# Score and value steps of a batch gathered into fewer visits, in banks borrowed from other stages

## The chip, the cores and the metric

One NeuronCore of a Trainium2 chip runs the whole kernel in one launch. The metric is the device time of that launch in microseconds; the median of several runs counts. The engines are named as in the profile: PE (TensorE) for matrix products and transposes, PEld for its weight loads, DVE (VectorE), ACT (ScalarE), POOL (GpSimd), and SP, whose queue issues most transfers.

## The reference

Two layers follow each other. The first is attention in a sliding window of 64 positions, causal, for 8 batches, 8 heads, 576 positions and a head size of 64. The second normalises the joined heads (512 wide), multiplies by two weight matrices with a relu between them, and adds its input.

```python
scores = scale * np.matmul(q, k.transpose(0, 1, 3, 2))
mask = (rel >= 0) & (rel < window)              # rel = query position - key position
attn = softmax(np.where(mask, scores, -1e9))
x = np.matmul(attn, v)                          # joined over heads: 8 x 576 x 512
xn = (x - mu) / np.sqrt(var + 1e-06) * g_ln
out = x + np.maximum(xn @ w_ch1, 0.0) @ w_ch2   # 512 -> 2048 -> 512
```

## The kernel before, in words

**Groups and stages.** The first 512 positions of each batch form a group of their own (groups 0 to 7); the last 64 positions of all eight batches, the tails, form group 8. For a group the second layer (the MLP) runs on TensorE in units: in groups 2 to 7 there are 16 units of the first layer (`l1`, L401: four matmuls of 128x512, then a relu on ScalarE, L405) and 14 half-products of the second layer (`stage`, L478: eight matmuls of 128x256 each). The second layer is computed with seven products instead of eight, in the order 1, 2, 6, 5, 7, 4, 3, two halves each. Product n's sums of the hidden values are made by VectorE (`s_sums`, L452), and what the products leave in three PSUM banks A, B and C is added by VectorE to the residual rows (`post`, L485). Bank A takes product 1, is added out, then takes product 6, is added out, then 7. Bank C lies in the transposing bank t1.

**The next batch's attention.** While the MLP of group g runs, the attention of batch g + 1 is computed in four blocks of 128 positions. For a block j there is a score step (`s_mm`): 16 matmuls (L286) on half of the rows of the array, into two PSUM banks, two exponentials on ScalarE (L294) and one multiplication by the mask on VectorE (`s_mask`, L301). Then a value step (`b_step`): 16 matmuls with 64 columns (L321) into a two-bank tile `xps`, and on VectorE a reciprocal (L324), a product (L327) and two statistics instructions (L329, L332). Then `z_step`: four GpSimd instructions (L351 to L354) that make the normalised rows z. Then `zt_step`: a transposing DMA on SP's queue (L362) or, for block 3 of batches 3 and 5, four transposes on TensorE (L366) and a copy on ScalarE. The tails have the same steps; in groups 3 and 5 one block of tails is handled, in group 7 two.

**Casts and transposes for the batch after that.** GpSimd casts the next but one batch's q and k to 16 bits (`cast_qk`, L128): in slot 11 two q casts and one k cast, in slot 16 the last k cast. The k casts are transposed on TensorE (`t_main`, L229, eight transposes each, through the banks t0 and t1, copied out by ScalarE at L215); the q casts are transposed by DMAs on SP's queue (L223). Then follow the casts of v (L147) and two DMAs issued by GpSimd that make a shifted copy of it.

**What sets the order.** The order is written out by hand. Each unit has a slot: after unit i has been issued, the calls registered for slot i are issued, in the order of registration. Every engine runs its own instructions in this order. The call `at(i, f, ...)` registers f in slot i. In groups 2 to 6 a batch's steps stand so (before):

- slot 27 of the group before: score step 0; slot 28: its mask
- slots 2, 7, 12: value step, rows and z of block 0, 1, 2, with score step 1, 2, 3 behind it; slots 3, 8, 13: masks
- slot 17: value step 3, its rows and z
- slots 1 and 5 in groups 3 and 5: score and value step of the tails
- slots 17 and 21 (18 and 22 in group 2): `t_main` for the two k casts
- slots 8 to 11 four `s_sums`, slots 13 to 15 six more, slots 19 and 21 one each

The PSUM has eight banks: two for scores (`sc`), two for the value step (`xps`), t0 and t1 for transposes, and two (`mm`) for the MLP, in which banks A and B lie as well.

Of the kernel before, what the change touches and what calls it, by code (L numbers as in the profile page):

```python
# [10 lines left out]
FP32 = mybir.dt.float32  # L11
# [4 lines left out]
ALU = mybir.AluOpType  # L16
# [4 lines left out]
def kernel(  # L21
# [10 lines left out]
    nc = tc.nc  # L32
    B, H, S, D = q.shape
# [3 lines left out]
    NGRP = B + 1  # L37
    NKC = DM // 128
    NHC = HID // 128
    NHP = H // 2  # L40
# [39 lines left out]
    tail32, tail16, tailT, vT = {}, {}, {}, {}  # L80
# [157 lines left out]
    def t_tail(i, x):  # L238
# [18 lines left out]
                    nc.tensor.transpose(out=tp[:, r, hp, :], in_=src[:, r, 2 * hp:2 * hp + 2, :], identity=ident16)  # L257
        evac(0, tailT[i][x], tp)

    def s_mm(g, j, pe_mask=False):  # L260
        sc = [ps_s.tile([128, NHP, 2, 64], FP32, tag="sc", name=f"sc_{g}_{j}_{par}") for par in range(2)]
        pt = p_pt.tile([128, 2, NHP, 2, 64], FP16, tag="pt", name=f"pt_{g}_{j}")
        pts[(g, j)] = pt
        if pe_mask:
            m = mbias[:, :]
            mb = bass.AP(tensor=m.tensor, offset=m.offset, ap=[m.ap[0], [0, NHP * 2], m.ap[1]])
            for par in range(2):
                nc.tensor.matmul(
                    out=sc[par][:, :].rearrange("p h w i -> p (h w) i"), lhsT=ident16, rhs=mb,
                    start=True, stop=False, skip_group_check=True,  # L270
                )
        for hp in range(NHP):
            for iw in range(2):
                for par in range(2):
                    rows = slice(64 * par, 64 * par + 64)
                    if g == NGRP - 1:
                        lhsT = tailT[j][1][rows, iw, hp, :]
                        rhs = tailT[j][0][rows, hp, 64 * iw:64 * iw + 64]
                    else:
                        w = 2 * j + iw  # L280
                        lhsT = qkT[g][1][rows, hp, 64 * w:64 * w + 128]
                        rhs = qkT[g][0][rows, hp, 64 * w:64 * w + 64]
                        if g >= XQ:
                            qb = flat(g)[rows, SM * hp + 16 * w:SM * hp + 16 * w + 16]
                            rhs = bass.AP(tensor=qb.tensor, offset=qb.offset, ap=[qb.ap[0], [128, 4], [1, 16]])
                    nc.tensor.matmul(out=sc[par][:, hp, iw, :], lhsT=lhsT, rhs=rhs,  # L286
                                     start=not pe_mask, stop=True, skip_group_check=pe_mask)

        for par in range(2):
            o, i = pt[:, par], sc[par][:, :]  # L290
            if XQ <= g < NGRP - 1:
                o = o.rearrange("p h w (r j) -> p (h w) r j", j=4)
                i = i.rearrange("p h w (j r) -> p (h w) r j", j=4)
            nc.scalar.activation(out=o, in_=i, func=AF.Exp, bias=0.0, scale=scale)  # L294
# [6 lines left out]
        nc.vector.tensor_tensor(out=ptv, in0=ptv, in1=mb, op=ALU.mult)  # L301

    def b_step(g, kb):
        kblk = f"{g}_{kb}"
        sfx, nb = ("r", 2) if g == NGRP - 1 else ("", None)
        if kb % 2 == 0:
            if (g, kb // 2) not in x_norm:
                for h in ((1, 0) if g // 2 == 2 else (0, 1)):
                    x_norm[(g, h)] = p_xn.tile([128, 2, DM], FP32, tag="xn" + sfx, name=f"xn_{g}_{h}", bufs=nb)
        xv = x_norm[(g, kb // 2)][:, kb % 2, :]  # L310
        xn = xv.rearrange("p (h d) -> p h d", h=H)
        xps = ps_x.tile([128, H, 128], FP32, tag="xps", name=f"xps_{kblk}")
        pt = pts.pop((g, kb))
        for h in range(H):
            par, hp = h % 2, h // 2
            for r in range(2):
                if sfx:
                    rhs = vT[kb][:, r, h, :]
                else:
                    rhs = (vA if r else vB)[g][:, kb, h, :]  # L320
                nc.tensor.matmul(out=xps[64 * r:64 * r + 64, h, :D + 1], lhsT=pt[:, par, hp, r, :], rhs=rhs,  # L321
                                 start=True, stop=True)
        rcp = p_blk.tile([128, H], FP32, tag="rcp", name=f"rcp_{kblk}")
        nc.vector.reciprocal(out=rcp, in_=xps[:, :, D])  # L324
        rcp_b = bass.AP(tensor=rcp.tensor, offset=rcp[:, :].offset,
                        ap=[rcp[:, :].ap[0], rcp[:, :].ap[1], [0, D]])
        nc.vector.tensor_tensor(out=xn, in0=xps[:, :, 0:D], in1=rcp_b, op=ALU.mult)  # L327
        stats = p_blk.tile([128, nc.vector.BN_STATS_DIM], FP32, tag="stats", name=f"stats_{kblk}")
        nc.vector.bn_stats(out=stats, in_=xv)  # L329
        if g not in mvg:  # L330
            mvg[g] = p_grp.tile([128, 4, 2], FP32, tag="mvg" + sfx, name=f"mvg_{g}", bufs=1 if sfx else 2)
        nc.vector.bn_aggr(out=mvg[g][:, kb, :], in_=stats)  # L332
        if g < 2 and (g, kb) != (0, 2):
            z_step(g, kb)
# [506 lines left out]
    for g in range(NGRP):  # L841
# [7 lines left out]
        def at(i, f, *a):  # L849
            slots[min(i, len(slots) - 1)].append((f, a))  # L850

        b = g + 1
        if g == 0:
            at(0, b_step, 0, 3)
# [28 lines left out]
        if g == 1:  # L883
            at(0, cast_qk, 2, 0)
            at(0, cast_qk, 2, 1)
            at(1, b_step, 1, 3)
            at(2, zt_step, 1, 2)
            at(13, newton, 1, 0, 4)
            at(5, zt_step, 1, 3)
            at(4, alloc_v, 2)  # L890
            at(4, alloc_qkT, 2)
            at(4, alloc_vB, 2)
            at(5, cast_v, 2, 0, 4)
            at(5, make_vB, 2)
            at(4, t_main, 2, 0, 0)
            at(4, t_main, 2, 1, 0)
            at(6, t_main, 2, 0, 1)
            at(6, t_main, 2, 1, 1)
            at(7, w2_sums, 3, 0, 4)
            at(8, w2_sums, 3, 4, 8)  # L900
            at(25, w2_sums, 2, 0, 4)
            at(28, w2_sums, 2, 4, 8)
            for j in range(4):
                at((9, 13, 16, 19)[j], s_mm, 2, j)
                at((10, 14, 17, 20)[j], s_mask, 2, j)
                at((14, 17, 20, 23)[j], b_step, 2, j)
                at((14, 17, 20, 23)[j], z_step, 2, j)
                at((18, 21, 24, 27)[j], zt_step, 2, j)
            at(3, load_qk, 3, 0)
            at(4, load_qk, 3, 1)  # L910
            at(7, load_v, 3, 0, 4)
            at(8, alloc_qkT, 3)
            at(8, cast_qk, 3, 0)
            at(10, cast_qk, 3, 1)
            at(14, alloc_v, 3)
            at(14, cast_v, 3, 0, 2)
            at(14, cast_v, 3, 2, 4)
            at(17, alloc_vB, 3)
            at(17, make_vB, 3)
            at(31, s_mm, 3, 0)  # L920
            at(31, s_mask, 3, 0)
            for i, (x, half) in zip((12, 24, 12, 28), ((0, 0), (1, 0), (0, 1), (1, 1))):
                at(i, t_main, 3, x, half, 0)
            at(40, load_qk, 4, 0)
            at(40, load_qk, 4, 1)
            at(40, load_v, 4, 0, 4)
# [4 lines left out]
        if g > 1 and g + 2 < B:  # L931
# [5 lines left out]
            else:  # L937
                at(11, cast_qk, g + 2, 0)
        if g > 1 and b < B:
            for j in range(4):  # L940
                if j:
                    at((2, 7, 12)[j - 1], s_mm, b, j)
                    at((3, 8, 13)[j - 1], s_mask, b, j)
                at((2, 7, 12, 17)[j], b_step, b, j)
                at((2, 7, 12, 17)[j], z_step, b, j)
                at((12, 12, 18, {3: 24, 5: 23}.get(b, 22))[j], zt_step, b, j)
        for n, i in enumerate(TAILS.get(g, ())):
            ts = (13, 13, 17, 22) if n else (1, 2, 5, 11)
            at(ts[0], s_mm, NGRP - 1, i)
            at(ts[1], s_mask, NGRP - 1, i)  # L950
            at(ts[2], b_step, NGRP - 1, i)
            at(ts[2], z_step, NGRP - 1, i)
            at(ts[3], zt_step, NGRP - 1, i)
        n = g + 2
        if g > 1 and n < B:
            at(16, cast_qk, n, 1, (1,) if n >= XQ else (0, 1))
            at(20, alloc_v, n)
            at(20, cast_v, n, 0, 2)
            at(21, cast_v, n, 2, 4)
            at(21, alloc_vB, n)  # L960
            at(21, make_vB, n)
            for i, (x, half) in zip((13, 18, 13, 22) if g == 2 else (13, 17, 13, 21),
                                    ((0, 0), (1, 0), (0, 1), (1, 1))):
                at(i, t_main, n, x, half, 0)
            at(27, s_mm, n, 0)
            at(28, s_mask, n, 0)
            if n + 1 < B:
                at(40, load_qk, n + 1, 0)
                at(40, load_qk, n + 1, 1)
                at(40, load_v, n + 1, 0, 4)  # L970
# [61 lines left out]
```

## Time and profile before

| | |
|---|---|
| times | 309.59 us median of three runs, 308.86 to 315.58 |
| span of the profiled execution | 305.9 us, from its first to its last instruction; no time of its own is given beside it |
| TensorE clock granted | 0.995 of full speed, mean over the span |
| DVE group L301 (masks) | 32 instructions, 27.5 us |
| DVE group L452 (sums) | 80 in all: 40 of them 24.5 us |
| POOL group L128 (q, k casts) | 32, 36.3 us, 1147 ns each |
| ACT group L405 (relus) | 104, 62.3 us, 599 ns each |
| ACT group L294 (exponentials) | 72, 39.0 us, 594 ns each |

How to read it: a busy time is the time that an engine spent in instructions, and says nothing yet about the end, since the engines run beside each other. The chain is the work followed back from the last instruction, each step to what released it. A group is all instructions of one line, engine and operation. In a timeline row stand the start from the beginning of the span, the length, the engine, the line, the operation and the tiles (out<-in); in square brackets the idle time ahead of it and what ended it. Rows that are merged show a count behind them.

### The profile page before, as it was taken

How to read it: one execution, taken by the hardware profiler on the slowest of the kernel's cores; microseconds unless marked ns; L12 is line 12 of the kernel's file. 1: busy time of each engine (PE TensorE's matmuls, PEld its weight loads, DVE VectorE, ACT ScalarE, POOL GpSimd, SP SyncE). 2: the span in 40 equal slices, each digit the busy share in tenths (PEclk: the TensorE clock that was granted, in tenths of full speed). 3: DMA queues.
4: the chain of work that ended last, by engine and by line, in shares of the span. 5: the costliest groups of instructions: out<-in, count | busy, mean ns of one | idle time of the engine just before them, and what ended most of it. 6: DMA issues, size and time to landing. Idle time of an engine off the chain costs nothing.

```text
span 305.9 us, 7582 instructions
## 1 busy us (share of the span) xinstructions
PE 295.4 (97%) x3061; PEld 196.4 (64%) x3061; DVE 220.6 (72%) x412; ACT 150.7 (49%) x253; POOL 173.3 (57%) x256
## 2 busy tenths in 40 slices
PE   6989999999999999999999999999999999999992
PEld 4557545687454478547854786469646854788882
DVE  0778696767766995589656965896669685789972
ACT  2586635587227733775157527752475046306500
POOL 7589676564952789179806983698146507014300
PEclk9999999999999999999999999999999999999998
DMA  8999999999776997899189997993790399003014
GB/s 191 266 385 301 314 366 286 303 284 236 150 181 228 243 172 147 280 280 127 35 243 303 204 160 245 298 155 70 215 175 19 53 189 208 19 17 139 0 38 103
DMA packets 113669, 58.35 MB, mean 191 GB/s; under 512 B 83617, under 2 KB 104609, under 8 KB 113634
## 3 DMA queue, kind: packets, MB, share of 16 engines
q1 hardware_dynamic: 112576, 54.67, 74.0%
q0 software_dynamic: 768, 2.80, 3.8%
q8 instruction: 24, 0.39, 0.5%
q10 hardware_dynamic: 290, 0.40, 0.5%
q14 instruction: 11, 0.09, 0.1%
HBM read 38.80 MB, written 9.44 MB: 158 GB/s over the span
## 4 chain that ended last, share of the span: by engine, by line
PE 89%; SPq 4%; DMA 2%; POOL 1%; ACT 1%; DVE 1%; issue 0%; ACTq 0%
PE hps L401 30%; PE pA L478 12%; PE pB L478 8%; PE pC L478 8%; PE hph L537 6%; PE ch L413 6%; PE xps L321 4%; PE sc L286 4%; PE ch L554 3%; PE tp L229 3%; PE lA L592 2%; DMA w1s<-in_moe_w_ch_dram 2%; SPq L141 2%; POOL w1g L190 1%; SPq L89 1%; PE lC L592 1%
## 5 line engine op out<-in xcount | busy, mean ns | idle before, releaser
L401 PE MATMUL hps<-zT,w1g 128*128 128x512 f16 x416 | 95.3, 380 | 0.0
L405 ACT ACTIVATE hrT<-hps 128x512 f16<-128x512 f32 x104 | 62.3, 599 | 39.3 <-PE hps L401 35.7
L401 PEld LDWEIGHTS <-w1g 128*128 128x128 f16 x416 | 38.6, 98 | 43.3 <-issue 0.7
L294 ACT ACTIVATE pt<-sc 128x512 f16<-128x512 f32 x72 | 39.0, 594 | 27.7 <-PE sc L286 20.5
L478 PEld LDWEIGHTS <-sS 128*128 128x128 f16 x448 | 43.4, 98 | 4.9
L351 POOL TENSOR_SCALAR rsz<-mvg 128x1 f32<-128x1 f32 x28 | 10.2, 364 | 60.6 <-DVE mvg L332 59.8
L128 POOL CAST qk<-qk 128x1024 f16<-128x1024 f32 x32 | 36.3, 1147 | 11.3 <-DMA qk<-in_k_dram 5.6
L478 PEld LDWEIGHTS <-hrT 128*128 128x128 f16 x336 | 32.4, 98 | 5.5 <-ACT hrT L637 0.3
L301 DVE TENSOR_TENSOR pt<-pt,mask 128x1024 f16<-128x1024 f16 x32 | 27.5, 867 | 8.4 <-ACT pt L294 8.4
L215 ACT COPY qkT<-tp 128x1024 f16<-128x1024 f16 x16 | 16.1, 1012 | 34.1 <-PE tp L229 34.1
L485 DVE TENSOR_TENSOR xn<-pA,xn 128x512 f32<-128x512 f32 x28 | 19.2, 685 | 16.7 <-PE pA L478 11.1
L478 PE MATMUL pC<-w2s,sS 128*128 128x256 f16 x224 | 27.1, 273 | 0.0
L478 PE MATMUL pA<-wT,sS 128*128 128x256 f16 x224 | 26.9, 273 | 0.0
L354 POOL TENSOR_SCALAR z<-xn,rsz 128x512 f16<-128x512 f32 x28 | 24.9, 888 | 2.9
L327 DVE TENSOR_TENSOR xn<-xps,rcp 128x512 f32<-128x512 f32 x36 | 24.9, 691 | 1.5 <-DMA out_dram<-xn 0.3
L329 DVE BATCH_NORM_STATS2 stats<-xn 128x6 f32<-128x512 f32 x36 | 25.0, 695 | 1.2
L324 DVE RECIPROCAL rcp<-xps 128x8 f32<-128x8 f32 x36 | 7.3, 204 | 24.7 <-PE xps L321 24.7
L452 DVE TENSOR_TENSOR sS<-hrT 128x512 f16<-128x512 f16 (+1 forms) x40 | 24.5, 613 | 0.6 <-ACT hrT L405 0.6
L537 PE MATMUL hph<-zT,w1g 128*128 128x256 f16 x192 | 23.8, 273 | 1.0 <-DVE zT L371 0.5
L321 PEld LDWEIGHTS <-pt 128*64 128x64 f16 x576 | 12.2, 110 | 13.7 <-issue 5.5
L352 POOL TENSOR_TENSOR rsz<-rsz,mhalf 128x1 f32<-128x1 f32 x28 | 19.4, 692 | 2.3
L147 POOL CAST vA<-v 128x1024 f16<-128x1024 f32 (+2 forms) x19 | 17.4, 930 | 5.6 <-DMA v<-in_v_dram 5.6
(113 smaller groups left out, 448.9 us busy)
## 6 DMA issues: line engine op xcount, KB each, us to landing
out_dram<-xn SPq DMA_DIRECT2D x33, 256.0 KB, 2.8
qk<-in_q_dram SPq DMA_DIRECT2D x16, 512.0 KB, 6.2
qk<-in_k_dram SPq DMA_DIRECT2D x16, 512.0 KB, 6.9
v<-in_v_dram SPq DMA_DIRECT2D x32, 256.0 KB, 7.7
w2s<-in_moe_w_ch_dram SPq DMA_DIRECT2D x9, 512.0 KB, 9.2
w1s<-in_moe_w_ch_dram SPq DMA_DIRECT2D x4, 512.0 KB, 7.3
tk<-in_k_dram SPq DMA_DIRECT2D x8, 256.0 KB, 4.5
tv<-in_v_dram SPq DMA_DIRECT2D x8, 256.0 KB, 5.0
```

What stands on the lines that cost most here:

```text
L128: nc.gpsimd.tensor_copy(out=dst[:, :].rearrange("p (a j) e d -> p a e j d", j=j), in_=t[:, :].rearrange("p (a e j d) -> p a e j d", e=2, j ...
L294: nc.scalar.activation(out=o, in_=i, func=AF.Exp, bias=0.0, scale=scale)
L301: nc.vector.tensor_tensor(out=ptv, in0=ptv, in1=mb, op=ALU.mult)
L321: nc.tensor.matmul(out=xps[64 * r:64 * r + 64, h, :D + 1], lhsT=pt[:, par, hp, r, :], rhs=rhs, start=True, stop=True)
L327: nc.vector.tensor_tensor(out=xn, in0=xps[:, :, 0:D], in1=rcp_b, op=ALU.mult)
L329: nc.vector.bn_stats(out=stats, in_=xv)
L354: nc.gpsimd.tensor_scalar(out=z, in0=xv, scalar1=rs, scalar2=nm, op0=ALU.mult, op1=ALU.add)
L401: nc.tensor.matmul(out=hps, lhsT=w1g[:, kc, 128 * hc:128 * (hc + 1)], rhs=zT[g][:, kc, :], start=(kc == 0), stop=(kc == NKC - 1),)
L405: nc.scalar.activation(out=hrT[:, hc, :], in_=hps, func=AF.Relu, bias=0.0, scale=1.0)
L452: nc.vector.tensor_tensor(out=o, in0=x, in1=y, op=op)
L478: nc.tensor.matmul(out=o, lhsT=a[:, c, 128 * p:128 * p + 128], rhs=wv[:, c, :], start=(first and (p == 0 or split_c) and c == 0), stop=(c ...
L537: nc.tensor.matmul(out=hps[:, e], lhsT=w1g[:, kc, 128 * hc:128 * (hc + 1)], rhs=zT[g][:, kc, 256 * half:256 * half + 256], start=(kc == 0) ...
```

## The change

The score step is split into its matmuls (`s_pe`) and its exponentials (`s_exp`, one or both halves); the value step into its matmuls (`b_pe`) and the VectorE instructions (`b_rows`). Both kinds of matmuls can now be given another home in PSUM: scores may lie in the two-bank `xps` tile or in t0 and t1, value steps in t0 and t1 or in the two score banks. Where a value step lies in two single banks, `b_rows` issues two reciprocals and two products of half the width.

In groups 2 to 6 the steps of the next batch are regrouped:

- slot 27 of the group before (slot 31, the end, in group 1): scores 0 and, in `xps`, scores 1; their four exponentials together; masks in slots 28 and 29 (in group 1 both in its last slot)
- slot 2: value step 0; scores 2; scores 3 (or the tail's) in t0 and t1, whose exponentials follow in slots 4 and 6 and whose mask follows in slot 6
- slot 8, without a tail: value steps 1 (`xps`), 2 (t0, t1) and 3 (score banks); rows of block 1 in slot 8, of block 2 in slot 12, of block 3 in slot 16, each with its z step
- slot 8, with a tail: value step 1 and the tail's (t0, t1), then scores 3; slot 12: value steps 2 (`xps`) and 3 (score banks); rows of the tail in slot 9
- the z transposes stand in slots 12, 14, 18 and 22 to 24, the second of them two slots later than before; the tail's in slot 14 and not 11

Group 7 with its two tail blocks keeps its order. In slot 16 the new calls are registered ahead of the last k cast.

```diff
+    def s_pe(g, j, pe_mask=False, home="sc"):
+        if home == "xps":
+            both = ps_x.tile([128, 2, NHP, 2, 64], FP32, tag="xps", name=f"sc_{g}_{j}")
+            sc = [both[:, par] for par in range(2)]
+        elif home == "t":
+            sc = [ps_t.tile([128, NHP, 2, 64], FP32, tag=f"t{par}", name=f"sc_{g}_{j}_{par}") for par in range(2)]
...
+    def b_pe(g, kb, home="xps"):
...
+        elif home == "t":
+            tiles = [ps_t.tile([128, H // 2, 128], FP32, tag=f"t{i}", name=f"xps_{kblk}_{i}") for i in range(2)]
+        else:
+            tiles = [ps_s.tile([128, H // 2, 128], FP32, tag="sc", name=f"xps_{kblk}_{i}") for i in range(2)]
...
+        for i, xps in enumerate(tiles):
+            nc.vector.reciprocal(out=rcp[:, n * i:n * i + n], in_=xps[:, :, D])
+        for i, xps in enumerate(tiles):
...
+            nc.vector.tensor_tensor(out=xn[:, n * i:n * i + n], in0=xps[:, :, 0:D], in1=rcp_b, op=ALU.mult)
...
+        def first_scores(b, i):
+            at(i, s_pe, b, 0)
+            at(i, s_pe, b, 1, False, "xps")
+            at(i, s_exp, b, 0, 0, 1)
+            at(i, s_exp, b, 1, 0, 1)
+            at(i + 1, s_mask, b, 0)
+            at(i + 2, s_mask, b, 1)
...
-            at(31, s_mm, 3, 0)
-            at(31, s_mask, 3, 0)
+            first_scores(3, 31)
...
+            tail = TAILS.get(g)
+            at(2, b_pe, b, 0)
+            at(2, b_rows, b, 0)
+            at(2, z_step, b, 0)
+            at(2, s_pe, b, 2)
+            at(2, s_exp, b, 2, 0, 1)
+            at(3, s_mask, b, 2)
+            if tail:
+                r, i = NGRP - 1, tail[0]
+                at(2, s_pe, r, i, False, "t")
+                at(4, s_exp, r, i, 0)
+                at(6, s_exp, r, i, 1)
+                at(6, s_mask, r, i)
+                at(8, b_pe, b, 1)
+                at(8, b_pe, r, i, "t")
+                at(8, s_mm, b, 3)
+                at(8, b_rows, b, 1)
+                at(8, z_step, b, 1)
+                at(9, s_mask, b, 3)
+                at(9, b_rows, r, i)
+                at(9, z_step, r, i)
+                at(12, b_pe, b, 2)
+                at(12, b_pe, b, 3, "sc")
+                at(14, zt_step, r, i)
+            else:
+                at(2, s_pe, b, 3, False, "t")
+                at(4, s_exp, b, 3, 0)
+                at(6, s_exp, b, 3, 1)
+                at(6, s_mask, b, 3)
+                at(8, b_pe, b, 1)
+                at(8, b_pe, b, 2, "t")
+                at(8, b_pe, b, 3, "sc")
+                at(8, b_rows, b, 1)
+                at(8, z_step, b, 1)
+            at(12, b_rows, b, 2)
+            at(12, z_step, b, 2)
+            at(16, b_rows, b, 3)
+            at(16, z_step, b, 3)
             for j in range(4):
-                if j:
-                    at((2, 7, 12)[j - 1], s_mm, b, j)
-                    at((3, 8, 13)[j - 1], s_mask, b, j)
-                at((2, 7, 12, 17)[j], b_step, b, j)
-                at((2, 7, 12, 17)[j], z_step, b, j)
-                at((12, 12, 18, {3: 24, 5: 23}.get(b, 22))[j], zt_step, b, j)
-        for n, i in enumerate(TAILS.get(g, ())):
+                at((12, 14, 18, {3: 24, 5: 23}.get(b, 22))[j], zt_step, b, j)
+        for n, i in enumerate(TAILS.get(g, ()) if b >= B else ()):
...
-            at(27, s_mm, n, 0)
-            at(28, s_mask, n, 0)
+            first_scores(n, 27)
```

## The prediction

> **What bounds the kernel now.** I read the page's totals and chain first, then one plain group (group 4) engine by engine in the timeline, then the waits.
>
> ```profile
> span 305.9 us, 7582 instructions
> PE 295.4 (97%) x3061; PEld 196.4 (64%) x3061; DVE 220.6 (72%) x412; ACT 150.7 (49%) x253; POOL 173.3 (57%) x256
> PE 89%; SPq 4%; DMA 2%; POOL 1%; ACT 1%; DVE 1%; issue 0%; ACTq 0%
> ```
>
> TensorE sets the time: 89% of the chain. In the stretches by group it is busy 31.49 of 31.50 us in group 4. So a microsecond less TensorE work is a microsecond gained only while every other engine keeps ahead of it. Next: what a visit costs, in the PE timeline (start, length).
>
> ```profile
> 158.61 4.49 PE L401 MATMUL hps<-zT,w1g 128*128 128x512 f16 x20
> 163.03 0.22 PE L321 MATMUL xps<-vB,pt 128*64 128x65 f16 x1
> ...
> 163.41 0.41 PE L286 MATMUL sc<-qkT,qkT 64*128 64x64 f16 x16
> 163.75 4.49 PE L401 MATMUL hps<-zT,w1g 128*128 128x512 f16 x20
> ```
>
> Twenty first-layer matmuls at 0.2157 (0.863 a unit) end at 162.93, so the value step starts 0.10 late; it holds PE for 0.38, the score step for 0.34. The pairs of value matmuls start 0.03 to 0.05 apart, so a step followed by another of its own shape costs 0.28. A change of shape costs about 0.10. Then how far ahead VectorE and GpSimd are, in their timelines:
>
> ```profile
> 165.31 0.66 DVE L301 TENSOR_TENSOR pt<-pt,mask 128x1024 f16<-128x1024 f16 x1
> 170.46 1.46 DVE L301 TENSOR_TENSOR pt<-pt,mask 128x1024 f16<-128x1024 f16 x1
> 171.84 1.25 DVE L452 TENSOR_TENSOR sS<-hrT 128x512 f16<-128x512 f16 x1
> 174.59 0.42 DVE L452 TENSOR_TENSOR sS<-sS,hrT 128x512 f16<-128x512 f16 x1
> 174.93 0.68 DVE L485 TENSOR_TENSOR xn<-pA,xn 128x512 f32<-128x512 f32 x1
> 175.53 0.20 DVE L324 RECIPROCAL rcp<-xps 128x8 f32<-128x8 f32 x1
> ```
>
> ```profile
> 165.49 0.54 POOL L351 TENSOR_SCALAR rsz<-mvg 128x1 f32<-128x1 f32 x1 [2.47 <-DVE mvg L332]
> 169.35 3.47 POOL L128 CAST qk<-qk 128x1024 f16<-128x1024 f32 x3
> 172.90 0.24 POOL L351 TENSOR_SCALAR rsz<-mvg 128x1 f32<-128x1 f32 x1
> 175.61 1.03 POOL L128 CAST qk<-qk 128x1024 f16<-128x1024 f32 x1
> 177.49 0.19 POOL L351 TENSOR_SCALAR rsz<-mvg 128x1 f32<-128x1 f32 x1 [0.85 <-DVE mvg L332]
> ```
>
> ```profile
> 175.92 1.91 PE L478 MATMUL pA<-wT,sS 128*128 128x256 f16 x16
> 177.67 0.61 PE L229 MATMUL tp<-ident,qk 128*128 128x128 f16 x8
> ```
>
> The margins are thin. VectorE adds bank A (post A) until 175.61; TensorE reuses that bank for product 6 at 175.92: 0.3 us. GpSimd ends the last k cast at 176.64; TensorE transposes it at 177.67: 1.0 us. The third of the casts at 169.35 ends at 172.82, its transposes start at 173.72: 0.9 us. And the row steps of block 3 (175.53) stand behind post A, its z step (177.49) behind the last k cast.
>
> **TensorE's part of the change.** A plain group before: three visits of 0.10 + 0.38 + 0.34, one value step of 0.48 and one score step of 0.44, 3.38 us. After: slot 2 0.10 + 0.38 + 0.28 + 0.34 = 1.10, slot 8 0.10 + 0.28 + 0.28 + 0.38 = 1.04, slot 27 0.72: 2.86. It saves 0.52 (groups 2, 4). A tail group goes from 4.30 (one score, one value visit more) to 1.10 + 1.10 + 0.76 + 0.72 = 3.68: 0.62 (groups 3, 5). Group 6 has no scores for a next batch: 0.80. Group 1's end gains a score step: 0.28. Sum: 2.8 us less, under 1%.
>
> **VectorE's part.** The four row instructions of a value step (reciprocal, product, two of statistics) take 1.79 (163.52 to 165.31). A step in two banks has two reciprocals and two products of 128x256: one more 0.20 and two of about 0.40 (0.419 at L489) for one of 0.69: 2.15, my estimate; bounds 1.79 and 2.25. Mask 1 leaves the layer-one stretch for slot 29, where VectorE waits anyway. But block 3's rows move from slot 17 to slot 16, and the unit of slot 17 issues post A: they now stand ahead of it.
>
> **GpSimd's part.** Its order was z0, z1, three casts, z2, last k cast, z3. With block 3's step in slot 16, registered before the cast of that slot, it is z0, z1, casts, z2, z3, last k cast. In tail groups the tail's z goes behind z1 and ahead of the casts. TensorE's transposes in slots 17 and 21 (18 and 22 in group 2) wait for those casts. The z transposes on SP move from slot 12 to 14 and behind the q ones; their issues are about 1.3 us each and the next group needs them 8 us later, so zero; if SP got stuck it would cost one issue.
>
> **Group 4, from its first matmul (155.17 = 0).** TensorE without waits: units 0 to 2 2.59, visit 1.10, units 3 to 8 to 8.87, visit to 9.91, units 9 to 15 to 15.95, products 1, transposes, 2, 6 (1.75 + 0.45 + 1.75 + 1.75) to 21.65; before, that point was 22.50. VectorE: value step 1 starts at 8.97, its reciprocal at 9.45 (0.49 after, as at 157.89 and 158.38), statistics ready at 11.25. Four sums 2.6: 13.85. Rows 2: 16.0. Six sums 3.09 (171.84 to 174.93): 19.1. Rows 3: 21.2. Post A 0.68: 21.9. Product 6 starts then and not at 19.9; before at 20.75. GpSimd: z1 starts at 11.25; z1, memset, casts, z2 ran without a gap from 165.49 to 175.66, 10.17: 21.4. z3 2.31 (177.49 to 179.80): 23.8. Last k cast 1.03: 24.8. So the transposes of slot 21 start at 24.9, 2.4 later than before. The casts for slot 17 end at 18.6 against an arrival at 17.7: a hole of 0.9 inside the same 2.4.
>
> Bounds: with sums at the quickest, 0.61 and 0.34, and the last two behind the last relu (16.8), rows 3 end at 20.0; with z at the quickest, 2.06 (195.56 to 197.62), the last cast ends at 23.1: +0.6. With z2 and z3 like z1, 3.66 (165.49 to 169.15): +4.6. I take the rows between, since they are of the same steps beside the same neighbours.
>
> **The other groups, in the same way.** Group 2 (transposes a unit later, in slot 22; VectorE's w2 sums put value step 1's rows 0.3 later): 25.1 against 23.54, +1.6. Tail groups 3 and 5: VectorE does rows 1, a sum, mask 3, then the tail's rows (to 14.7); its z ends at 17.3, the casts (3.73) at 21.1, z2 23.9, rows 3 at 23.5, z3 26.2, the cast 27.2, against 147.46 - 124.03 = 23.43: +3.8 each. Group 6 has no casts; post A alone: 21.5 against 20.3, +1.2. After those points the stages run as before, with one more score step in slot 27: 0.28 for groups 1 to 5, 1.4.
>
> **ScalarE.** Four exponentials in a row instead of two; their starts are 0.51 apart.
>
> ```profile
> 92.60 1.08 ACT L294 ACTIVATE pt<-sc 128x512 f16<-128x512 f32 x2 [1.91 <-PE sc L286]
> 93.63 0.60 ACT L405 ACTIVATE hrT<-hps 128x512 f16<-128x512 f32 x1
> ```
>
> At the end of group 1 the first relu of group 2 waits behind them: exps from 0.44 after the scores start, relu from 2.48 to 3.08, while unit 2 could start at 0.62 + 1.73 = 2.35: 0.8 once. In groups 2 and 4 the copy of the tail's q transposes ends at 3.1 after the scores start, and slot 29's transposes, which reuse the bank, arrive at 2.6: 0.5 each, 1.1 in all; bounds 0 and 1.6 (one product stage more or less). The late exps of slots 4 and 6 fit between relus (0.49 + 0.51 of 0.863: 0.14 late at most; taken as zero).
>
> **Sum.** 1.6 + 3.8 + 2.4 + 3.8 + 1.2 + 1.4 + 0.8 + 1.1 = +16.1; the saved 2.8 is inside. The profiled span is 305.9 and no own time is given for that execution; the median of the three times is 309.59, so 3.7 lies around the span. 309.6 + 16.1 = **325.7 us**.
>
> **A rule against the trace.** A mask took 0.66 at 165.31 and 1.46 at 170.46, a sum 0.42 and 1.25: the long ones lie in the casts of 169.35 to 172.82. The Trainium skill, "SBUF — State Buffer", "Who interferes with whom", says why: a VectorE instruction with two SBUF inputs and a GpSimd one that reads SBUF exclude each other for a whole instruction. By it the six sums, which now fall into the casts, would get two done by 18.7 and end at 20.1 and not 19.1: rows 3, z3 and the cast 0.8 later in groups 2 to 5, and 328.9 in place of 325.7.
>
> **Rivals.**
> 1. Quick rows: GpSimd's and VectorE's steps run undisturbed (the lower bounds above). Then group 2 stands even, group 4 at +0.6, the tail groups at +2.0 (rows 3 to 22.3, z3 and the cast to 25.4 against 23.43), group 6 at +0.4; with 1.4, 0.8 and 1.1: +8.3, **318**. For it: z at 2.06 exists, beside VectorE's row steps. Against: z1 and z2 run beside its sums.
> 2. Not slower: GpSimd and VectorE keep up, and TensorE's 2.8 stays, less ScalarE's 1.9: **308.7**. It decides where GpSimd needs 10.4 us from value step 1's statistics to the last k cast (11.25 to 21.65). For it: GpSimd is busy for only 20.8 of group 4's 31.5 us. Against: the rows give 13.6, the quickest ones 11.9.
> 3. Worse: every z like z1, 3.66: group 2 +3.8, group 4 +4.6, tails +7.2 each, the rest as forecast: +27, **337**. For it: z1 takes 3.66 in each of groups 2 to 5. Against: no z2 or z3 does.
>
> No row shows what a TensorE hole does to its clock, granted at 1.00 from 92.5 to 300. The Trainium skill, "TensorE: Matmul & The Clock Gate", "What's actually happening", puts the window at about 3.4 us idle, and my longest hole is 2.6 (slot 17 of a tail group, 18.5 to 21.1); were it passed in both tail groups, 3.4 us at half rate would add 1.7 each, 329.1.
>
> **Numbers.** Forecast 0.63, rival 1 0.16, rival 2 0.12, rival 3 0.09. The forecast's own range is 320 to 331; for 8 in 10 I reach past rival 1, to 315, and to 334, which leaves out rival 2 and most of rival 3. Two per cent, 6.2 us, is about what a measurement of this kernel tells from no change: faster 0.02 (an edge of rival 2), same 0.12 (the rest of it and an edge of rival 1), slower 0.86.
>
> **What would show it.** In group 4: holes in PE before the transposes of slots 17 and 21 (released by GpSimd's cast) and before product 6 (released by the add of bank A), together 3 us or more; block 3's reciprocals ahead of that add; the last k cast behind z3; three stretches of small matmuls at 1.10, 1.04 and 0.72. A PE still busy 31 of 31 us would show me wrong: then the queues had room that I don't see. Holes only at product 6 would be rival 1.

## The result, and the profile after

| | before | after |
|---|---|---|
| median | 309.54 us (308.86 to 315.58, 6 runs) | 325.25 us (324.7 to 326.7, 6 runs) |
| profiled execution: span | 305.9 us | 324.8 us (its own time 326.7) |

The changed kernel takes 1.052 times as long (95% interval 1.049 to 1.056), 15.7 us more. Ratios are taken from the runs within 1.5% of their kernel's fastest; medians and ranges, here and below, are of all runs.

The page of after, its totals and its chain:

```profile
span 324.8 us, 7607 instructions
...
PE 298.9 (92%) x3061; PEld 197.6 (61%) x3061; DVE 223.3 (69%) x432; ACT 150.2 (46%) x253; POOL 167.7 (52%) x256
...
PE 60%; DVE 20%; SPq 5%; DMA 5%; ACT 3%; issue 3%; POOL 3%; POOLq 0%; DVEq 0%
```

TensorE has as many instructions as before, but its share of the chain fell from 89% to 60%, and VectorE's rose from 1% to 20%: TensorE now waits. Where, the stretches from one group's first first-layer matmul to the next show (columns: stretch, its length, then the busy time of each engine with its count, TensorE's granted clock, DMA share, GB/s). Groups 2 to 6 of after:

```profile
94.58:130.70 36.12, 32.90 (x342) 21.76 (x337) 26.02 (x51) 18.27 (x32) 20.91 (x31) 0.95 0.84 185
130.70:166.32 35.62, 32.64 (x355) 21.29 (x353) 23.71 (x48) 17.21 (x29) 19.32 (x31) 0.95 0.64 153
166.32:200.97 34.65, 31.37 (x339) 20.82 (x337) 22.94 (x46) 16.73 (x29) 20.15 (x31) 1.00 0.85 213
200.97:236.55 35.58, 31.13 (x355) 20.46 (x353) 23.72 (x48) 17.21 (x29) 19.27 (x31) 1.00 0.62 154
236.55:265.74 29.19, 28.39 (x275) 18.75 (x273) 20.19 (x43) 11.57 (x21) 12.49 (x20) 1.00 0.52 121
```

Groups 4 and 6 of before, beside them:

```profile
155.17:186.53 31.36, 31.35 (x339) 21.03 (x337) 22.31 (x42) 16.67 (x28) 20.84 (x31) 1.00 1.02 229
217.82:246.86 29.04, 29.04 (x290) 19.09 (x288) 20.13 (x40) 12.49 (x22) 12.63 (x20) 1.00 0.56 117
```

In before the five stretches are 31.37, 31.30, 31.36, 31.29 and 29.04 long, and TensorE is busy in all but 0.02 of each. The groups are longer by 4.75, 4.32, 3.29, 4.29 and 0.15: 16.8 us. Group 7 to the end is the same (59.06 and 59.04). The profiled execution of after also begins group 2 2.1 us later; experiment 8, the kernel before once more, says how far that can be put down to the change.

TensorE's holes in the second half of group 4 (its timeline; in brackets the idle time and what ended it):

```profile
184.90 0.62 PE L229 MATMUL tp<-ident,qk 128*128 128x128 f16 x8 [0.66 <-POOL qk L128]
...
188.72 1.91 PE L514 MATMUL pA<-wT,sS 128*128 128x256 f16 x16 [1.45 <-DVE xn L521]
...
191.47 0.62 PE L229 MATMUL tp<-ident,qk 128*128 128x128 f16 x8 [0.84 <-POOL qk L128]
```

These are the three places of the forecast: the transposes of slot 17 behind GpSimd's casts, product 6 behind the add of bank A, the transposes of slot 21 behind the last k cast. The two queues that end them, VectorE and then GpSimd, in group 4 of after:

```profile
181.99 0.77 DVE L488 TENSOR_TENSOR sS<-hrT 128x512 f16<-128x512 f16 x1
182.80 1.14 DVE L488 TENSOR_TENSOR sS<-sS,hrT 128x512 f16<-128x512 f16 x1
183.87 1.25 DVE L488 TENSOR_TENSOR sS<-hrT 128x512 f16<-128x512 f16 x1
185.04 0.41 DVE L488 TENSOR_TENSOR sS<-hrT,sS 128x512 f16<-128x512 f16 x1
...
186.16 0.24 DVE L359 RECIPROCAL rcp<-xps 128x4 f32<-128x4 f32 x2
...
187.99 0.67 DVE L521 TENSOR_TENSOR xn<-pA,xn 128x512 f32<-128x512 f32 x1
```

```profile
181.45 3.39 POOL L128 CAST qk<-qk 128x1024 f16<-128x1024 f32 x3
...
188.16 0.19 POOL L387 TENSOR_SCALAR rsz<-mvg 128x1 f32<-128x1 f32 x1 [0.92 <-DVE mvg L368]
...
189.45 0.98 POOL L390 TENSOR_SCALAR z<-xn,rsz 128x512 f16<-128x512 f32 x1
190.38 1.03 POOL L128 CAST qk<-qk 128x1024 f16<-128x1024 f32 x1
```

Block 3's rows (186.16 to 187.99) stand ahead of the add of bank A (L521, 187.99). z3 waits 0.92 for those rows, and the last k cast (190.38) stands behind z3. The first three of the six sums are slow, 0.77, 1.14 and 1.25, exactly while the casts run (181.45 to 184.84); the other three take 0.4 each.

One thing the forecast did not have. In group 2 product 6 waits 2.33 us, and the matmuls behind that hole run at a granted clock of 0.50 and not 1.00 (stretches of TensorE alone: stretch, length, busy time, granted clock, DMA share, GB/s):

```profile
117.80:119.00 1.20, 1.20 (x6) 0.52 1.03 195
119.00:121.20 2.20, 2.20 (x13) 0.50 0.52 105
```

### The profile page after: what moved, and what is told of

It is laid out like the page before. It is cut to its first block, busy times and chain, and to the rows that moved or that the text cites. A ratio compares the mean times of both kernels' runs of the same rounds, so it can differ in the third digit from the quotient of the medians.

```text
span 324.8 us, 7607 instructions
## 1 busy us (share of the span) xinstructions
PE 298.9 (92%) x3061; PEld 197.6 (61%) x3061; DVE 223.3 (69%) x432; ACT 150.2 (46%) x253; POOL 167.7 (52%) x256
## 4 chain that ended last, share of the span: by engine, by line
PE 60%; DVE 20%; SPq 5%; DMA 5%; ACT 3%; issue 3%; POOL 3%; POOLq 0%; DVEq 0%
PE hps L437 17%; PE pA L514 8%; DVE sS L488 7%; PE pC L514 7%; PE ch L449 4%; PE pB L514 4%; SPq L141 4%; DVE xn L363 3%; DVE stats L365 3%; DMA v<-in_v_dram 3%; PE hph L573 3%; PE ch L590 2%; PE xps L343 2%; DMA vB<-vA 2%; PE lA L628 2%
## 5 line engine op out<-in xcount | busy, mean ns | idle before, releaser
L437 PEld LDWEIGHTS <-w1g 128*128 128x128 f16 x416 | 39.1, 98 | 45.9 <-issue 2.8
L387 POOL TENSOR_SCALAR rsz<-mvg 128x1 f32<-128x1 f32 x28 | 10.6, 378 | 80.4 <-DVE mvg L368 79.7
L514 PEld LDWEIGHTS <-sS 128*128 128x128 f16 x448 | 44.2, 100 | 12.5 <-issue 6.7
L128 POOL CAST qk<-qk 128x1024 f16<-128x1024 f32 x32 | 34.9, 1104 | 13.5 <-DMA qk<-in_k_dram 7.0
L215 ACT COPY qkT<-tp 128x1024 f16<-128x1024 f16 x16 | 16.1, 1012 | 49.8 <-PE tp L229 49.7
L316 DVE TENSOR_TENSOR pt<-pt,mask 128x1024 f16<-128x1024 f16 x32 | 23.7, 742 | 21.7 <-ACT pt L309 21.6
L514 PEld LDWEIGHTS <-hrT 128*128 128x128 f16 x336 | 33.3, 100 | 6.2 <-ACT hrT L673 0.3
L521 DVE TENSOR_TENSOR xn<-pA,xn 128x512 f32<-128x512 f32 x28 | 19.2, 685 | 25.6 <-PE pA L514 25.6
L514 PE MATMUL pA<-wT,sS 128*128 128x256 f16 x224 | 28.5, 283 | 6.0 <-DVE xn L521 6.0
L488 DVE TENSOR_TENSOR sS<-hrT 128x512 f16<-128x512 f16 (+1 forms) x40 | 25.9, 647 | 0.6 <-ACT hrT L441 0.6
L363 DVE TENSOR_TENSOR xn<-xps,rcp 128x512 f32<-128x512 f32 (+1 forms) x46 | 25.5, 573 | 0.9
L390 POOL TENSOR_SCALAR z<-xn,rsz 128x512 f16<-128x512 f32 x28 | 22.7, 809 | 2.9
L229 PE MATMUL tp<-ident,qk 128*128 128x128 f16 x176 | 14.1, 229 | 7.5 <-POOL qk L128 7.5
L573 PEld LDWEIGHTS <-w1g 128*128 128x128 f16 x192 | 17.9, 98 | 3.0 <-DVE zT L407 0.7
```

Source lines behind the costliest of these rows:

```text
L128: nc.gpsimd.tensor_copy(out=dst[:, :].rearrange("p (a j) e d -> p a e j d", j=j), in_=t[:, :].rearrange("p (a e j d) -> p a e j d", e=2, j ...
L363: nc.vector.tensor_tensor(out=xn[:, n * i:n * i + n], in0=xps[:, :, 0:D], in1=rcp_b, op=ALU.mult)
L390: nc.gpsimd.tensor_scalar(out=z, in0=xv, scalar1=rs, scalar2=nm, op0=ALU.mult, op1=ALU.add)
L437: nc.tensor.matmul(out=hps, lhsT=w1g[:, kc, 128 * hc:128 * (hc + 1)], rhs=zT[g][:, kc, :], start=(kc == 0), stop=(kc == NKC - 1),)
L488: nc.vector.tensor_tensor(out=o, in0=x, in1=y, op=op)
L514: nc.tensor.matmul(out=o, lhsT=a[:, c, 128 * p:128 * p + 128], rhs=wv[:, c, :], start=(first and (p == 0 or split_c) and c == 0), stop=(c ...
```

## The experiments

All variants but number 8 are edits of the kernel after, and none leaves out a part of the result. "Group 2 to 6" are lengths between first first-layer matmuls, as above. The kernel before, beside them on the same chips, had medians of 308.9 to 309.6.

**1. The last k cast ahead of z3.**

```diff
-            at(16, cast_qk, n, 1, (1,) if n >= XQ else (0, 1))
+            at(15, cast_qk, n, 1, (1,) if n >= XQ else (0, 1))
```

> The changed kernel with one step moved: the last k cast stands in slot 15, so ahead of block 3's z on GpSimd; everything else as changed. Theory (two queues are late, GpSimd's casts and VectorE's add of bank A): the holes ahead of slot 21's transposes (0.83, 0.84, 0.85 us in groups 3, 4, 5) close, the holes ahead of product 6 (2.33, 1.45, 1.45, 0.80) and of slot 17 (2.15, 0.66, 2.15) stay: about 2.5 us less, 322.7. Rival (GpSimd's order costs nothing, VectorE alone is late): 325.2, and slot 21 still waits for something else.

Measured 322.19 (320.98 to 324.75), ratio 1.043 [1.037, 1.049]; 3.1 us off, for 2.5 expected. All holes of slot 21 are gone, and those of slot 17 stayed. Product 6 still waits 2.33, 1.45 and 0.79 in groups 2, 4 and 6; in group 5 its 1.45 is missing; there the granted clock fell to 0.50 just ahead of it (more on that below). So z3 ahead of the last k cast cost about what its holes say; the 0.6 beyond them is less than these runs differ by.

**2. Block 3's rows and z back in slot 17.**

```diff
-            at(16, b_rows, b, 3)
-            at(16, z_step, b, 3)
+            at(17, b_rows, b, 3)
+            at(17, z_step, b, 3)
```

> The changed kernel with the rows and the z step of block 3 back in slot 17, behind the add of bank A on VectorE and behind the last k cast on GpSimd. Theory: the holes ahead of product 6 and of slot 21 close, and group 2's product 6 no longer runs at a clock of 0.5 after a hole; the holes of slot 17 stay. Counted from the trace of the changed kernel: 2.3 + 1.7 in group 2, 0.8 in 3, 2.3 in 4 and 5, 0.8 in 6, about 10 us less: 315. Rival (the six sums are what is late, and the add comes late behind them anyway): under 4 us less, and a hole ahead of product 6 stays.

Measured 314.64 (314.08 to 316.33), ratio 1.019 [1.014, 1.023]; 10.6 us off. In group 2, where the hole was 2.33, VectorE now reads:

```profile
114.81 0.68 DVE L521 TENSOR_TENSOR xn<-pA,xn 128x512 f32<-128x512 f32 x1
115.41 0.24 DVE L359 RECIPROCAL rcp<-xps 128x4 f32<-128x4 f32 x2
```

The add (114.81) is ahead of the reciprocals, and product 6 waits 0.51. The holes of product 6 in groups 4 to 6 and those of slot 21 are gone as well, since z3 is again behind the last k cast. The groups take 32.64, 32.94, 32.12, 32.95, 28.23. In the two profiles these groups differ by 12.3 us (3.48, 2.68, 2.53, 2.63 and 0.96): the holes of product 6 in after (2.33, 1.45, 1.45, 0.80, less the 0.51 that is left), those of slot 21 (0.83, 0.84, 0.85), the half clock, about 1.6 each in groups 2 and 3 (it fell nowhere in this profile), and about 1 us that holes cost beyond their length. The medians differ by less, 10.6, since the profiled execution of after was its longest and this one among the shortest of its kernel. The place of one step, rows and z together, holds two thirds of the loss. The edit moves two things; experiment 1 undid the second alone, the last k cast behind z3, and gained 3.1, so the larger part is the rows ahead of the add. The holes of slot 17 (2.15, 0.66, 2.15) are untouched.

**3. The three casts ahead of z1.**

```diff
-                at(11, cast_qk, g + 2, 0, (0,))
-                at(11, cast_qk, g + 2, 1, (0,))
-                at(11, cast_qk, g + 2, 0, (1,))
+                at(8, cast_qk, g + 2, 0, (0,))
+                at(8, cast_qk, g + 2, 1, (0,))
+                at(8, cast_qk, g + 2, 0, (1,))
```

> The changed kernel with the three casts of slot 11 moved to slot 8, ahead of the z of block 1 (and of the tails' z). Theory: the holes of slot 17 close (2.15, 0.66 and 2.15 us, and the half clock after the one in group 3); the six sums no longer fall into the casts and take about 2.2 us in place of 4.1, so that product 6 and slot 21 are earlier too: 7 us less, 318. Rival (the sums are long for another reason than the casts beside them): only slot 17's holes go and return ahead of product 6: 2 us less, 323. Second rival (q and k have not landed in slot 8): the casts wait for their transfers and delay the z steps, no gain.

Measured 320.54 (319.03 to 324.52), ratio 1.034 [1.030, 1.038]; its profiled execution, 324.5, is the longest of its runs. The holes of slot 17 are gone. The six sums of group 4 (VectorE's timeline) show what the casts did to them:

```profile
180.51 0.39 DVE L488 TENSOR_TENSOR sS<-hrT 128x512 f16<-128x512 f16 x1
180.94 0.43 DVE L488 TENSOR_TENSOR sS<-sS,hrT 128x512 f16<-128x512 f16 x1
181.28 0.42 DVE L488 TENSOR_TENSOR sS<-hrT 128x512 f16<-128x512 f16 x1
```

All six end 2.23 us after their start; beside the casts, in after, it was 4.17 (181.99 to 186.16). The profile of experiment 7, where the casts stand in the same place, shows 2.24 (173.92 to 176.16). So the first rival is out. But the move brought waits of its own: in group 4 the casts wait 0.84 for q's transfer and hold z1 back. Product 6 waits only 0.35 there, for 1.45 in after, but still 1.67 to 1.81 in groups 2, 3 and 5, where block 3's rows stand ahead of the add as in after. In group 4 of this longest execution z3 also waits 1.61 for its buffer, and the transposes of slot 21 come 2.33 late. What of this the other runs have, and so why it is 320.5 and not 318, is not shown.

**4. The second exponentials of the first scores one slot later.**

```diff
-            at(i, s_exp, b, 1, 0, 1)
+            at(i + 1, s_exp, b, 1, 0, 1)
...
-            first_scores(3, 31)
+            first_scores(3, 30)
```

> The changed kernel with the exponentials of scores 1 one slot later (behind the copy of the tail's q), and in group 1 both first score steps one slot earlier. Theory: the waits behind four exponentials in a row go (0.57 us at group 2's third unit, 0.32 ahead of the tail's k transposes in groups 2 and 4): 1.2 us less, 324.0. Rival (a later mask of block 1 delays VectorE's adds at the end of the group): 325.2 or more.

Measured 323.33 (322.38 to 324.3), ratio 1.046 [1.042, 1.050]; 1.9 us off, for 1.2 expected. TensorE's waits for ScalarE, 0.57 in group 2 and 0.32 before groups 3 and 5, are gone.

**5. Edits 2 and 4 together.**

> Block 3's rows and z back in slot 17, and the second exponentials of the first scores one slot later, the first scores of batch 3 in slot 30 of group 1. Theory (each hole of TensorE costs its own length): to rows3_slot17's 314.6 the later exponentials take away ScalarE's 0.57 and two of 0.32: 313.4. The three holes before the transposes of slot 17 (2.15, 0.66, 2.15) stay, and groups 3, 4, 5 stay at 32.9, 32.1, 32.9. Rival (the exponentials only shift a wait that something else sets): 314.6.

Measured 313.77 (313.1 to 314.49), ratio 1.015 [1.012, 1.017]; the time is as expected, but group 3 is not. The groups take 31.71, 34.62, 31.64, 32.96, 28.23. Groups 3 and 5 have the same hole before slot 17, 2.15 and 2.16; in group 3 the clock fell to 0.50 behind it, in group 5 it stayed at 1.00, and they differ by 1.66.

**6. The same, and the k transposes two slots and one slot later.**

```diff
-            for i, (x, half) in zip((13, 18, 13, 22) if g == 2 else (13, 17, 13, 21),
+            for i, (x, half) in zip((13, 18, 13, 22) if g == 2 else (13, 19, 13, 22),
```

> As rows17_exps_later, and in groups 3 to 6 the k transposes of slots 17 and 21 two slots and one slot later (19 and 22). Theory: GpSimd is late only against the slot where its casts are asked for; the casts end 2.15 us after the start of slot 17 in tail groups, and two product units (3.5 us) lie between slot 17 and slot 19, so the holes of 2.15, 0.66 and 2.15 go: 313.4 - 5.0 = 308.5, even with the kernel before or 1 below. Rival: the late casts also push what stands behind them (the last k cast, the next group's first exponentials), and 1 to 3 us of the 5 come back in slot 22 or at the next group's head: 310 to 312.

Measured 313.64 (312.04 to 314.14), ratio 1.013 [1.010, 1.017]: nothing gained, and neither account is right. In group 5 TensorE's holes are now these:

```profile
213.24 0.62 PE L229 MATMUL tp<-ident,qk 128*128 128x128 f16 x8 [0.41 <-POOL qk L128]
215.24 1.91 PE L514 MATMUL pA<-wT,sS 128*128 128x256 f16 x16 [1.38 <-DVE xn L521]
```

Without the wait for GpSimd, product 6 arrives 1.6 us earlier (21.5 and not 23.1 into group 5), and the add of bank A is not done: VectorE's six sums take 4.25 beside the casts in a tail group (144.11 to 148.36 in group 3). The wait of 2.15 became one of 0.41 and one of 1.38; the 0.2 that this saves in group 5 (32.76 for 32.96) is all. Group 3, with the same two holes, takes 34.42 because the clock fell there. My theory had named the late engine and forgotten the next one, equally late and covered by the first. VectorE is late because the casts lie on its sums, and where TensorE asks for the casts does not change that.

**7. All three edits 2, 3 and 4.**

> Block 3's rows and z in slot 17, the three casts in slot 8 ahead of z1, the second exponentials later. Theory: every hole named so far has lost its cause (rows ahead of the add of bank A, casts behind z1, exponentials ahead of the relu), so what is left is TensorE's own sum with fewer changes of shape: 308, 1 to 2 us below the kernel before. Rival: the casts in slot 8 wait 0.8 for q's transfer and put z1 and z2 some 2 us later, z3 and the last k cast then miss slot 21 by 0.9 to 2.3 as in casts_slot8, and the time stays at 311 to 313.

Measured 309.96 (307.9 to 313.23), ratio 1.001 [0.996, 1.006]: the whole loss is gone, though the median is 2 us above the theory's 308. The groups of the profiled execution take 31.46, 30.75, 31.31, 31.64, 28.24. The holes of slot 21 seen in edit 3 alone did not come, which speaks against the rival. One larger hole is left, 0.85 ahead of product 6 in group 5. It goes back to a transfer: the casts waited 1.76 for q, so they ran into mask 3 (first VectorE, then GpSimd), which took 1.52, and VectorE was late from there on. Experiments 9 and 10 try this account.

```profile
200.01 1.52 DVE L316 TENSOR_TENSOR pt<-pt,mask 128x1024 f16<-128x1024 f16 x1
```

```profile
198.43 2.56 POOL L128 CAST qk<-qk 128x1024 f16<-128x1024 f32 x2 [1.76 <-DMA qk<-in_q_dram]
```

**8. The kernel before once more.** One run.

> The kernel before, unchanged, for a second profile. Groups 0 and 1 are the same code before and after until the end of group 1, yet the scores of batch 3 begin at 92.16 in the profile of before and at 94.0 in that of after. If this is how one execution differs from another, this profile can have them anywhere from 92 to 95; if the change moved something in the early loads, they are at 92.2 again.

310.54 us, span 308.7. The first matmul of group 2 stands at 95.28, not 92.5, and from there to the end it takes 213.42, against 213.40. So groups 0 and 1 differ from one execution to the next by 2.8 us, and the rest hardly at all: the 2.1 us by which after began group 2 later are nothing that the change is shown to have done. Most of the 2.8 is one hole in group 1: TensorE waits 2.34 (until 76.53) for VectorE, whose mask at 70.45 took 3.31 beside three casts of GpSimd (70.20 to 73.21). In before the same mask began at 70.07, ahead of the next cast (70.34), and took 0.69. The steadiest reading of an edit is therefore the time from group 2's first matmul to the end: 213.4 before, 230.2 after, 212.4 with all three edits.

**9. All three, and q and k loaded earlier.**

```diff
-                at(40, load_qk, n + 1, 0)
-                at(40, load_qk, n + 1, 1)
+                at(26, load_qk, n + 1, 0)
+                at(26, load_qk, n + 1, 1)
```

The two loads for batch 4 in group 1 go from slot 40 to 29 in the same way.

> As all_three, with the loads of the next batch's q and k issued some slots earlier, in slot 26 of the group before (slot 29 in group 1) and not at its end. Theory: the two waits left over in all_three for q's transfer (0.81 and 1.76 on GpSimd in groups 3 and 5) go, the casts end before mask 3, which takes 0.66 again in place of 1.52, and the hole of 0.85 ahead of product 6 in group 5 goes with it: about 1 us under all_three, groups 5 near 30.75, and 211.4 in place of 212.4 us from group 2's first matmul to the end. Rival: the loads, issued earlier, only stand in SP's queue for their buffers or hold back the z transposes behind them, and the next group begins later: no gain, or 1 us lost.

Measured 313.58 (311.52 to 316.92), ratio 1.013 [1.010, 1.017]: 3.6 worse than experiment 7. The waits for q in groups 3 and 5 are gone as the theory had it, and mask 3 of group 5 takes 0.68; product 6 still waits 0.49 to 0.79 in groups 3 to 5, and the rest of the loss is in a place that neither theory named. The three casts now run without a gap after z0 in groups 3 and 5, but the copies that make v's shifted rows, issued by GpSimd at 153.92 and 154.51 ahead of group 4, come late, and the first value step of the group waits:

```profile
161.32 0.19 PE L343 MATMUL xps<-vB,pt 128*64 128x65 f16 x1 [1.37 <-DMA vB<-vA]
```

The larger of the two copies (KB, then us from issue to landing), in this kernel and in the one of experiment 7:

```profile
vB<-vA POOLq DMA_DIRECT2D x1, 260.0 KB, 7.3
```

```profile
vB<-vA POOLq DMA_DIRECT2D x1, 260.0 KB, 2.9
```

The smaller one, of 195 KB, took 8.5 and 5.0.

**10. All three, and the loads one pair of output stores earlier.** For batches 5 to 7:

```diff
-                at(40, load_qk, n + 1, 0)
-                at(40, load_qk, n + 1, 1)
+                at(28, load_qk, n + 1, 0)
+                at(28, load_qk, n + 1, 1)
```

> As all_three, with the loads of q and k for batches 5 to 7 one pair of output stores earlier (slot 28). In all_three_early_loads the value rows' copies on GpSimd's queue took 7.3 and 8.5 us from issue to landing beside the loads, 2.9 and 5.0 in all_three without them, and TensorE waited 0.40, 1.37 and 1.66 for them at slot 2. Theory: what matters is whether the loads lie on those copies; one pair of stores earlier is 1 to 2 us, the copies are nearly down by then: no wait at slot 2 over 0.3, q's waits on GpSimd 1 us shorter, group 5's hole of 0.85 smaller: 309 to 310, 0 to 0.8 under all_three. Rival: any earlier issue already delays the copies: 311 or more, with a wait at slot 2 of groups 3 and 5.

Measured 308.96 (306.08 to 311.55), ratio to before 0.997 [0.994, 1.001], at the lower edge of what the theory gave. The copies took 2.9 and 4.8, no hole came at slot 2, and the hole of 0.85 is gone. Its groups 2 to 6 take 31.35, 30.74, 31.06, 30.74, 28.23; of groups 3 and 4 the stretches are:

```profile
125.24:155.98 30.74, 30.74 (x355) 20.61 (x353) 22.17 (x50) 17.21 (x29) 19.76 (x31) 1.00 0.75 181
155.98:187.04 31.06, 30.88 (x339) 20.89 (x337) 21.16 (x45) 16.74 (x29) 20.04 (x31) 1.00 1.01 234
```

From group 2 on the kernel takes 211.2 (305.1 less 93.89), against 213.4 in both profiles of before: 2.2 us less. TensorE's holes in these groups are down to 0.29 (mask 3 in group 2) and 0.18 (a z transpose in group 4). The whole time can't be told from before with certainty, since the interval reaches just past 1: groups 0 and 1 vary by more than the regrouping is worth.

## Why the prediction came out right, point by point

The forecast was 325.7 and the median is 325.25. The mechanism was the one named: holes at slot 17, at product 6 and at slot 21, block 3's reciprocals ahead of the add, the last k cast behind z3, and experiments 2, 1 and 3 remove them one by one. That the sum came within half a microsecond is in part luck: errors of opposite sign in group 6 and the clock, and in the six sums and the rows, cancel. By groups:

| group | forecast (its own terms) | profile of after |
|---|---|---|
| 2 | 0.8 + 1.6 + 0.28 + 0.5 = 3.2 | 4.75, of it about 1.6 the half clock |
| 3 | 3.8 + 0.28 = 4.1 | 4.32 |
| 4 | 2.4 + 0.28 + 0.5 = 3.2 | 3.29 |
| 5 | 3.8 + 0.28 = 4.1 | 4.29 |
| 6 | 1.2 | 0.15 |
| sum | 15.8 (1.1 for ScalarE not rounded); 16.1 with group 1's 0.28 | 16.8 |

- **TensorE's part.** In groups 2 to 6, 3.1 us was to be saved (the 2.8 is less the 0.28 that group 1 gains). Where the waits are gone (experiment 10), 2.2 are, with two holes of 0.5 together left in groups 2 and 4: these give 0.02 and 0.30 for 0.52, groups 3 and 5 give 0.56 and 0.55 for 0.62, group 6 gives 0.81 for 0.80. The three visits of group 4 in after take about 1.08, 1.10 and 0.67, for 1.10, 1.04 and 0.72. In after all of it lay inside the waits, as the sum had it.
- **The six sums.** The step "Six sums 3.09 (171.84 to 174.93): 19.1" was too short: 4.17, to 19.84. The rule that was set against the row, from the Trainium skill, "SBUF — State Buffer", "Who interferes with whom", put their end at 20.1. Here the measurement lies nearer the page's rule than the row: 4.17 beside the casts, 2.23 without them in experiment 3, though three sums, and not two, were done by 18.8. The 328.9 that went with the rule did not come, for the reason in the next point. The row of before that I used instead was one in which the casts lay on only part of the sums.
- **The rows.** "2.15, my estimate" for a step in two banks was too long: 1.83 (186.16 to 187.99). This and z2 (2.3 for 2.76) made up for most of the sums: last k cast's end 25.1 for 24.8, transposes of slot 21 at 25.15 for 24.9.
- **Group 6.** "+1.2" failed. No casts run there, so its six sums took 2.23 (252.22 to 254.45), not 3.09, and its split rows 0.3 less each. Product 6 started at 20.46, not 21.5; the hole of 0.80 is what the fewer visits save, and the group is 0.15 longer.
- **ScalarE.** "0.8 once" measured 0.57, "0.5 each" 0.32 each. Experiment 4 took 1.9 us off for these 1.2; the rest is within the difference between runs.
- **The clock.** I held that a hole of up to 2.6 us would leave it at 1.00. Behind holes of 2.33 and 2.15 it didn't: see below. In group 2 the drop cost 1.6. In group 3, behind the 2.15 before slot 17, it cost nothing: while TensorE ran slowly, VectorE caught up, and the 1.45 that product 6 waits in group 5 is missing in group 3 (4.32 and 4.29). So groups 2 to 6 without the clock are 15.2 (16.8 less 1.6), for 15.8 forecast: group 6 was 1 too long, and the clock, which the forecast had left out, put 1.6 back.
- **The rivals.** "Not slower" decided at GpSimd needing 10.4 us from value step 1's statistics to the last k cast. It needed 13.6 in group 4 (177.83 to 191.41), as the forecast's rows had it. Experiments 7 and 10 show the other side of that point: with another order on the same engines the regrouping does no harm, and the 2.2 us appear.

What stays open: why holes cost more than their length. TensorE's busy time in after, beside that of experiment 10, is 0.16 longer in group 6 with one hole (28.39 and 28.23), 0.39 in group 5 with three (31.13 and 30.74) and 0.49 in group 4 with four (31.37 and 30.88). Open is also why groups 0 and 1 vary, but for the one hole of experiment 8.

## What to carry to other kernels

When steps of one stage are gathered, look first at what they now stand ahead of in the in-order queues: here one row step of VectorE one slot too early, ahead of an add that freed a PSUM bank, and the GpSimd step behind it, ahead of a cast, held two thirds of a 5% loss, while TensorE's own saving was under 1%. A hole that is closed uncovers the next late engine, so ask why each is late: the waits at slot 17 and at product 6 of the tail groups went together only when the casts moved off the sums, not when TensorE asked for them later. Before a transfer is issued earlier, ask which others it will then run beside: the loads of q and k 7 to 10 us earlier, measured from the issue of two small copies, delayed these by about 4 us; 2 to 3 us earlier, still behind that issue, they did not.

## What was unexpected of the hardware

**The clock.** Behind 8 of 14 holes of 2.14 to 2.33 us, over the profiles of after and its variants, the granted clock fell to 0.50 for 3.41 us; behind 6 of the same length it stayed at 1.00. The Trainium skill, "TensorE: Matmul & The Clock Gate", "What's actually happening", gives one idle window of about 3.4 us for the fall. The measurement decides: here 2.1 us can be enough.

The granted clock recorded in the traces shows what decides between the 8 and the 6. In all twelve profiles every change of the clock stands a whole number of steps of 3.413 us after its first rise to 1.00 (31, 32, 41, 42 and 91 steps in after; the first rise lies between 8.97 and 12.04 us). The 8 holes, and one of 2.10 in group 1 of experiment 3, each lie whole inside one such step, and the clock fell at that step's end, 0.06 to 1.06 us after the hole. The 6 others, and the one of 2.34 in experiment 8, are cut by a step's end into two parts, the longer of 1.32 to 1.82 us. In after the hole from 149.44 to 151.59 (group 3) has the next step's end behind it, at 151.99: the clock fell there. The hole from 219.71 to 221.86 (group 5) has a step's end inside it, at 220.26: the clock stayed.

Behind single holes of 1.81 or less, more than twenty, it never fell. Once it fell after 0.41 and 1.38 with eight transposes between them, which lie together in one step (group 3 of experiment 6); in group 5 a step's end cuts the second of the same pair, and the clock stayed. So the edge lies near 1.8 us of idle time in one step. It is not sharp in these records: three steps with 1.80 to 1.82 kept the clock and this one with 1.79 lost it, and the ends of matmuls are modelled. Where a hole falls in the step was chance here, so equal holes can differ by 1.6 us from one execution to the next (groups 3 and 5 of experiment 5).

**Transfers beside each other.** Two copies of 260 and 195 KB took 2.9 and 5.0 us from issue to landing, and 7.3 and 8.5 when four loads of 512 KB were issued on another queue ahead of them and beside them (the loads from 152.74 to 154.46, the copies at 153.92 and 154.51, in experiment 9). With the first load 3.2 us behind the first copy, in experiment 10, they took 2.9 and 4.8.
